# A Fourier mixing layer and a maxout FFN on one core: batches 0 and 1 in a new order, yb read in 4 transfers, last stores on two queues

## The chip, the cores and the metric

The kernel runs on one core of a Trainium2 chip. The metric is device time in microseconds (us). TensorE is called PE, its weight loads PEld; VectorE is DVE, ScalarE is ACT, GpSimd is POOL, SyncE is SP. A line such as L344 is a line of the kernel before.

## What is computed

```python
X = np.fft.fft(x, axis=1)            # x: (8, 3072, 256), float32
X = np.fft.fft(X, axis=2)
t = X.real.reshape(8 * 3072, 256)
h = np.maximum(np.maximum(t @ w1, t @ w2), t @ w3)   # w1, w2, w3: 256 x 768
out = h @ w_out                                      # w_out: 768 x 256
```

Eight batches of 3072 rows; the weights are shared.

## The kernel before, in words

Everything is written out in one order for each engine by hand (`manual_schedule`, L67); the framework adds only the waits. Each engine, and each engine's queue of DMA issues, works strictly in that order. A DMA also waits for the DMA eight before it of its kind, whose semaphore it takes over.

**Mixing.** The class `Mix` (L332) turns one batch of x into two bf16 tables tE and tO (128 x 1536), the even and odd parts of the transform along the sequence.
- `load_x` (L106) fetches x into one of two tiles xt, from POOL's queue, which also casts float32 to bf16; `mirror` (L113) then copies the reversed columns to partitions 64 to 127 with two DVE copies (L116, L117).
- `s(k)` (L340), k = 0 to 6: two matmuls with the small table tabz (L344; L348 for k = 6), evicted into tb (L346, L350).
- `y` (L352) stores tb to a DRAM tile db, in two or more pieces, two DMAs each. `z` (L361) reads it back transposed into yb: three parts, two column sets, and for each one DMA for row 48 and one for rows 0 to 47, so 12 DMAs. There is one yb; a read waits for all use of the batch before.
- `x0` (L375) computes a small correction x0s, and `c` (L384) copies it into yb (L385), after the reads have landed; on POOL, except for the first copy of batch 0, which is on ACT.
- `k(which, g)` (L387): matmuls of yb with the tables te_tab or to_tab (L395), evicted into tE (which = 0, called kE) or tO (kO) (L397). kO needs `c`, kE does not. `end` (L399) adds the last column.

**FFN.** gE, gO, gD are products of the DFT along the features and the weights (`product` L278, `keep_product` L290), so the FFN starts from tE and tO. A batch has 18 units: 3 blocks of 512 columns by 6 slices of the hidden width. In a unit `unit_plus` (L406) runs four 128x512 matmuls into two banks (L412, L413), `unit_out` (L423) takes the maximum of three (ACT stmp L426, DVE hp L427), and one unit later `unit_minus` (L416, L420) adds the gD products and a second `unit_out` gives hm. The second layer of a block (`l2_block`, L440; matmuls L436, L459, sum on DVE L464) is spread over the next six units; half of its rows go out with an indirect DMA on POOL (L469), half with DMAs on SP (L476). The last block has a form of its own, `l2_last` (L479), stored at L509.

**Order.** Before the units comes a start written line by line (L129 to L594): tables on POOL, DVE and ACT, batch 0's x in four chunks (FIRST, L127), its mixing, the first half of the products, and dummy matmuls `warm_up` (L555) that keep PE busy. From then on the dictionary `plan` (L623) says which mixing step runs behind which unit: `at(b, unit, fn)`. `fetch` and `turn` are loads and mirrors of a later batch; `ahead0`, `ahead1` and `ahead` (L671 to L677) place the steps of batch 1, batch 2 and the later ones within the units of the batch before. Before the change the start and the plan have it so:

```python
    for ch in range(4):
        at(0, (7, 8, 10, 11)[ch], lambda ch=ch: turn(1, ch))
        at(0, (12, 13, 14, 15)[ch], lambda ch=ch: fetch(2, ch))
        at(1, (1, 2, 3, 4)[ch], lambda ch=ch: turn(2, ch))
...
    ahead0 = {8: ("s0", "s1"), 9: ("s2", "y0"), 11: ("s3", "s4"), 12: ("s5", "s6", "y1", "x"),
              13: ("z",), 16: ("c",), 17: ("kE0", "kO0"), 20: ("kE1",), 21: ("kO1",),
              24: ("kE2",), 25: ("kO2", "end")}
```

Weights: `load_w(0)` (L252) is issued on POOL after the tables and fetches the first half of w1, w2, w3; `load_w(1)`, wout and batch 1's x follow after the fourth read of yb (L588 to L594).

Of the kernel before, what the change touches and what calls it, by code (L numbers as in the profile page):

```python
# [9 lines left out]
FP32 = mybir.dt.float32  # L10
# [33 lines left out]
def kernel(  # L44
# [9 lines left out]
    nc = tc.nc  # L54
# [77 lines left out]
    arv = ang_r.rearrange("p (k r) -> p k r", r=RI)  # L132
# [4 lines left out]
    dvec = gen.tile([128, 128], FP32, tag="dvec")  # L137
    iota(dvec, [[1, 128]])
    for i in range(2):
        nc.gpsimd.memset(xt[i][32:64, 0::48, :], 0.0)  # L140
    for (s0, s1) in FIRST:
        for h in range(2):
            load_x(0, s0, s1, h)

    kvec = gen.tile([128, NHALF + 1], FP32, tag="kvec")
    kv = kvec[:, 0:NHALF].rearrange("p (g c) -> p g c", g=3)
    for g in range(3):
# [10 lines left out]
         base=S + 1023, cm=-32)  # L158

# [4 lines left out]
    nc.vector.memset(yb, 0.0)  # L164
# [4 lines left out]
    half = gen.tile([128, 256], FP32, tag="half")  # L169
    nc.vector.memset(half[:, 0:128], 64.0)  # L170
    nc.vector.memset(half[:, 128:256], 0.0)

# [68 lines left out]

    def load_w(jh, after=None):
        ld = None
        for wsrc, wdst in ((moe_w1, w1_bf), (moe_w2, w2_bf), (moe_w3, w3_bf)):
            ld = nc.gpsimd.dma_start(
                out=wdst.rearrange("p (fc j) -> p fc j", fc=2)[:, :, jh * 384:(jh + 1) * 384],
                in_=wsrc.rearrange("(fc p) j -> p fc j", fc=2)[:, :, jh * 384:(jh + 1) * 384])
            if after is not None:
                tc.add_manual_dep(ld.ins, after.ins.name, AFTER, reason="others first")
        return ld  # L250

    load_w(0)  # L252

    scal(sgn, pidx, 0.0, ALU.is_equal)
    scal(sgn, sgn, 2.0, ALU.mult, -1.0, ALU.add)
    scal(dif, sgn, 1.0, ALU.subtract)
    angles(0, 512)
    mirror(0, *FIRST[1])
    nc.gpsimd.memset(x0s, 0.0)

    rows_v = rows_f.rearrange("p (b r) -> p b r", r=12)
    adj = gen.tile([128, 12], FP32, tag="adj")
    adv = adj.rearrange("p (g u) -> p g u", u=4)
    three = pidx.to_broadcast([128, 3])
    for u in (1, 2, 3):
        scal(adv[:, :, u], three, float(128 - 32 * u), ALU.is_ge, 3071.0, ALU.mult)
    low = gen.tile([128, 4], FP32, tag="low")
    for i, (edge, value) in enumerate(((31.0, -1023.0), (16.0, -1520.0), (32.0, -522.0),
                                       (32.0, -1541.0))):
        scal(low[:, i:i + 1], pidx, edge - 0.5, ALU.is_le, value, ALU.mult)  # L270
    scal(adv[:, 0, 0:1], low[:, 0:1], -32.0, ALU.add)
    nc.vector.tensor_tensor(out=adv[:, 1, 0:1], in0=low[:, 1:2], in1=low[:, 2:3], op=ALU.add)
    dve(out=adv[:, 2, 0:1], in_=low[:, 3:4])
    nc.vector.tensor_tensor(out=rows_v, in0=rows_v,
                            in1=adj.unsqueeze(1).to_broadcast([128, B, 12]), op=ALU.add)
    dve(out=rows_m, in_=rows_f)
# [55 lines left out]
    class Mix:  # L332
# [28 lines left out]
        def z(self, parts=(0, 1, 2), engs=(nc.sync, nc.sync)):  # L361
            spans = {0: ((0, 6, 0), (1, 6, 17)), 1: ((6, 12, 6), (6, 11, 22)),
                     2: ((12, 17, 12), (12, 17, 27))}
            done = []
            for part in parts:
                for cs in range(2):
                    (i0, i1, c0) = spans[part][cs]
                    c1 = c0 + i1 - i0
                    for (a, z) in ((48, NS), (0, 48)):
                        done.append(engs[cs].dma_start(  # L370
                            out=yb[cs * 64 + a:cs * 64 + z, i0 * 256:i1 * 256],
                            in_=self.db[a:z, c0 * 256:c1 * 256]))
            return done
# [13 lines left out]
        def k(self, which, g):  # L387

            special = {0: [(0, 0, 32)], 1: [(0, 0, 16), (16, 16, 16)], 2: [(16, 0, 32)]}[g]
            parts = [(5 * g + 1 + i, 32 + 96 * i, 96) for i in range(5)] + special  # L390
            tab = (te_tab, to_tab)[which]
            ps2 = ps_f.tile([128, 512], FP32, name="ps2", tag="ps")
            for (r, c0, wd) in parts:
                at = 11 if r == 16 else r if r < 11 else r + 1
                nc.tensor.matmul(ps2[:, c0:c0 + wd], ybv[:, at, which, :],  # L395
                                 tab[:, g * 512 + c0:g * 512 + c0 + wd], start=True, stop=True)
            nc.scalar.copy(out=(self.tE, self.tO)[which][:, g * 512:(g + 1) * 512], in_=ps2)  # L397
# [81 lines left out]
    def l2_last(hp, hm, te, to, flipped):  # L479
# [3 lines left out]
        for sub in (3, 0, 1, 2):  # L483
# [23 lines left out]
            for k, (p0, p1, row, c) in enumerate(stores):  # L507
                eng = nc.scalar if sub == 2 and k < 2 else nc.sync
                stored(eng.dma_start(out=out[row: row + 32 * (p1 - p0 - 1) + 1: 32, :],  # L509
                                     in_=ot[p0:p1, c:c + 256]), "direct", ("scattered",))  # L510
# [52 lines left out]
    nc.scalar.activation(out=md_all, in_=vm, func=AX.Sin, scale=float(2.0 * math.pi / 256.0))  # L563
    nc.scalar.activation(out=nmd_all, in_=vm, func=AX.Sin, scale=float(-2.0 * math.pi / 256.0))
# [3 lines left out]
    mirror(0, *FIRST[2])  # L568
    tables(0, 512)
    warm_up(4)  # L570
    m.s(4, pool=ps_s, evict=dve)
    m.y(32, 40)
    mirror(0, *FIRST[3])
    m.s(5, pool=ps_s)
    m.s(6, pool=ps_s, evict=dve)
    m.y(40, NS, engs=(nc.sync, nc.scalar))
# [48 lines left out]
    def at(b, unit, fn):  # L625
        plan.setdefault((b + unit // UNITS, unit % UNITS), []).append(fn)
# [27 lines left out]
    for (u, fn) in ((0, lambda: tables(1024, NHALF + 1)), (0, lambda: m.c(6, RI)),  # L654
                    (1, prep_some), (2, prep_some), (2, prep_some), (2, prep_some),
                    (3, lambda: m.k(0, 1)), (3, prep_some), (4, lambda: m.k(1, 1)),
                    (4, prep_some), (5, prep_some), (5, prep_some),
                    (7, lambda: m.k(0, 2)), (8, lambda: m.k(1, 2)), (8, m.end)):
# [12 lines left out]
    ahead0 = {8: ("s0", "s1"), 9: ("s2", "y0"), 11: ("s3", "s4"), 12: ("s5", "s6", "y1", "x"),  # L671
              13: ("z",), 16: ("c",), 17: ("kE0", "kO0"), 20: ("kE1",), 21: ("kO1",),
              24: ("kE2",), 25: ("kO2", "end")}
    ahead1 = {3: ("s0", "s1"), 4: ("s2", "y0", "s3"), 5: ("s4", "s5"), 6: ("s6", "y1", "x"),
              9: ("z",), 12: ("c",), **late}
    ahead = {1: ("s0", "s1"), 2: ("s2", "y0", "s3"), 3: ("s4", "s5"), 4: ("s6", "y1", "x"),
             7: ("z",), 11: ("c",), **late}  # L677
    for b in range(B - 1):
        for u, whats in (ahead0, ahead1, ahead)[min(b, 2)].items():
            for what in whats:  # L680
                at(b, u, lambda b=b, what=what: piece(b + 1, what))
# [75 lines left out]
```

## Time and profile before

| what | us |
|---|---|
| median of 3 runs (lowest, highest) | 450.39 (447.83, 450.78) |
| the profiled execution | 451.0 |
| its span, first to last instruction | 449.2 |
| PE busy in the span | 406.6 (91%) |
| DVE, ACT, POOL busy | 296.1, 255.2, 155.1 |
| mean granted PE clock | 0.984 |

The span is what the views divide; 1.8 us of the execution lie outside it. "Busy" of PE counts modelled ends of pipelined matmuls. A line of the timeline gives start, duration, engine, line of the kernel, operation, tiles (out<-in) and shape, and in brackets the idle time ahead of it with what ended it. "SPq", "ACTq" and "POOLq" are the queues' issues, which do not count as busy; "x12" means twelve instructions merged in one line, whose duration runs from the first start. The wait list gives total us, how often, and the longest.

### The profile page before, as it was taken

What the parts mean: (1) busy time and instruction counts of PE and PEld (TensorE: products, weight loads), DVE (VectorE), ACT (ScalarE), POOL (GpSimd) and SP (SyncE); (2) the same over time, 40 slices, a digit from 0 to 9 for tenths busy, and PEclk for the clock granted to TensorE, in tenths of its full rate; (3) what the DMA queues carried; (4) which work ended last, traced back from release to release, by engine and by line L of the source; (5) the groups of instructions that cost most, each with busy time, mean ns of one, the idle gap of its engine ahead of it and who ended that gap; (6) DMA issues with size and microseconds to landing.
All of it is one profiled execution on the core that took longest, in us unless ns stands there. A gap on an engine that the chain in (4) does not pass through costs nothing.

```text
span 449.2 us, 8328 instructions
## 1 busy us (share of the span) xinstructions
PE 406.6 (91%) x2768; PEld 250.8 (56%) x2768; DVE 296.1 (66%) x527; ACT 255.2 (57%) x481; POOL 155.1 (35%) x263
## 2 busy tenths in 40 slices
PE   1488889599987999999998999999999999999994
PEld 0144555355654666665665566665666566656663
DVE  6766775447564767685677667676669577666772
ACT  1457556247654665666656665666566755745540
POOL 9145033222252214531435125332443233214330
PEclk9999999869998999999999999999999999999999
DMA  7849246912496236943397257924693354312323
GB/s 105 132 105 193 36 101 132 209 38 80 92 189 139 70 98 143 207 110 84 98 187 160 73 137 153 183 90 103 146 205 92 83 132 123 91 49 59 85 82 107
DMA packets 68875, 52.79 MB, mean 118 GB/s; under 512 B 35816, under 2 KB 62960, under 8 KB 68320
## 3 DMA queue, kind: packets, MB, share of 16 engines
q0 software_dynamic: 23856, 26.28, 29.7%
q1 hardware_dynamic: 44544, 25.78, 22.7%
q8 instruction: 22, 0.36, 0.4%
q10 hardware_dynamic: 432, 0.20, 0.2%
q14 instruction: 21, 0.17, 0.1%
HBM read 34.73 MB, written 31.59 MB: 148 GB/s over the span
## 4 chain that ended last, share of the span: by engine, by line
PE 70%; DMA 11%; DVE 7%; issue 4%; ACT 3%; SPq 2%; POOL 1%; DVEq 0%; ACTq 0%; POOLq 0%
PE po L436 22%; PE pse L412 12%; PE pse L420 11%; PE pse L413 11%; DMA yb<-db 5%; PE ps L344 5%; PE po L459 3%; DMA xt<-in_x_dram 3%; DMA out_dram<-ot 3%; ACT stmp L426 2%; DVE hm L427 2%; PE pl L451 2%; PE ps L395 2%; SPq L476 1%; DVE ot L464 1%
## 5 line engine op out<-in xcount | busy, mean ns | idle before, releaser
L426 ACT ACTIVATE stmp<-pse 128x512 bf16<-128x512 f32 x288 | 170.1, 600 | 85.9 <-PE pse L413 73.7
L469 POOL DMA_INDIRECT out_dram<-ot,rows_m x92 | 105.4, 1146 | 234.2 <-DVE ot L464 219.2
L427 DVE TENSOR_TENSOR hp<-pse,stmp 128x512 bf16<-128x512 f32 x144 | 99.6, 691 | 114.8 <-PE pse L420 70.7
L412 PE MATMUL pse<-tE,gE 128*128 128x512 bf16 x288 | 110.0, 382 | 3.1 <-DVE hm L427 2.4
L413 PE MATMUL pse<-tO,gO 128*128 128x512 bf16 x288 | 110.0, 382 | 0.1
L427 DVE TENSOR_TENSOR hm<-pse,stmp 128x512 bf16<-128x512 f32 x144 | 99.1, 688 | 9.2 <-ACT stmp L426 8.2
L436 PE MATMUL po<-wout_bf,hp 128*128 128x256 bf16 x576 | 87.3, 275 | 0.0
L420 PE MATMUL pse<-tO,gD 128*128 128x512 bf16 x288 | 86.6, 382 | 0.0
L436 PE MATMUL po<-wout_bf,hm 128*128 128x256 bf16 x576 | 78.6, 273 | 0.0
L436 PEld LDWEIGHTS <-hp 128*128 128x128 bf16 x576 | 57.0, 99 | 27.0 <-issue 0.5
L436 PEld LDWEIGHTS <-hm 128*128 128x128 bf16 x576 | 56.4, 98 | 16.3
L464 DVE TENSOR_TENSOR ot<-po,even 128x512 f32<-128x512 f32 x92 | 62.9, 684 | 0.2
L420 PEld LDWEIGHTS <-gD 128*128 128x128 bf16 x288 | 27.8, 98 | 32.3 <-issue 0.5
L344 PE MATMUL ps<-xt,tabz 128*128 128x512 bf16 x96 | 27.5, 403 | 18.7 <-DVE xt L117 17.8
L346 ACT CAST tb<-ps 128x512 bf16<-128x512 f32 x47 | 25.9, 588 | 30.5 <-PE ps L344 30.5
L413 PEld LDWEIGHTS <-gO 128*128 128x128 bf16 x288 | 28.2, 98 | 26.5 <-issue 5.9
L412 PEld LDWEIGHTS <-gE 128*128 128x128 bf16 x288 | 28.2, 98 | 23.0 <-issue 1.7
L459 PE MATMUL po<-gw,tO 128*128 128x512 bf16 x92 | 35.4, 385 | 0.0
L397 ACT CAST tO<-ps 128x512 bf16<-128x512 f32 x24 | 14.1, 586 | 24.0 <-PE ps L395 12.9
L455 ACT COPY even<-pl 128x512 f32<-128x512 f32 x46 | 26.9, 585 | 0.9 <-PE pl L451 0.9
L116 DVE COPY xt<-xt 64x1524 bf16<-64x1524 bf16 (+4 forms) x32 | 19.1, 596 | 9.4 <-DMA xt<-in_x_dram 5.6
L397 ACT CAST tE<-ps 128x512 bf16<-128x512 f32 x24 | 14.1, 587 | 19.4 <-PE ps L395 19.4
(132 smaller groups left out, 233.6 us busy)
## 6 DMA issues: line engine op xcount, KB each, us to landing
out_dram<-ot SPq DMA_DIRECT2D x75, 96.0 KB
xt<-in_x_dram POOLq DMA_DIRECT2D x14, 384.0 KB
db<-tb SPq DMA_DIRECT2D x21, 192.0 KB
yb<-db SPq DMA_DIRECT2D x32, 120.0 KB
out_dram<-ot SPq DMA_DIRECT2D x48, 64.0 KB
xt<-in_x_dram POOLq DMA_DIRECT2D x7, 400.0 KB
xt<-in_x_dram POOLq DMA_DIRECT2D x7, 368.0 KB
yb<-db SPq DMA_DIRECT2D x16, 144.0 KB
```

The costliest lines, as they stand in the source:

```text
L344: nc.tensor.matmul(ps1, tab_at[hh], self.x[:, 8 * k + hh:8 * k + 8:2, 0:128], start=(hh == 0), stop=(hh == 1))
L397: nc.scalar.copy(out=(self.tE, self.tO)[which][:, g * 512:(g + 1) * 512], in_=ps2)
L412: nc.tensor.matmul(pse[:, 0:n], gE[i][:, js], te, start=True, stop=False)
L413: nc.tensor.matmul(pse[:, 0:n], gO[i][:, js], to, start=False, stop=True)
L420: nc.tensor.matmul(pse, gD[i][:, js], to, start=False, stop=True, skip_group_check=True)
L426: nc.scalar.activation(out=stmp[:, 0:n], in_=pses[0][:, 0:n], func=AX.Relu)
L427: nc.vector.tensor_tensor(out=dst, in0=src3, in1=stmp[:, 0:n], op=ALU.max)
L436: nc.tensor.matmul(po, hcols(jc), wout_bf[:, jc * 256:(jc + 1) * 256], start=False, stop=(jc == NJC - 1), skip_group_check=True)
L455: nc.scalar.copy(out=even, in_=pl)
L459: nc.tensor.matmul(po, to[:, cp], gw[:, 256:768], start=True, stop=True)
L464: nc.vector.tensor_tensor(out=ot.rearrange("p (h c) -> p h c", h=2), in0=po.rearrange("p (h c) -> p h c", h=2), in1=lin.unsqueeze(1).to_br ...
L469: stored(nc.gpsimd.indirect_dma_start(out, bass.IndirectOffsetOnAxis(ap=rows_m[0:128 - lo, b * 12 + slot: b * 12 + slot + 1], axis=0), ot[ ...
```

## The change

Seven things, all in order or grouping; the matmuls of the units stay as they are.

1. ang_r is filled by two iotas instead of four (yb now has its columns in natural order); the zeroing of two columns of xt moves from POOL to DVE; dvec's iota moves behind the first chunk's loads; the zeroing of yb moves on DVE to just before the first mirror.
2. Both halves of the weights are issued on POOL right behind x: the first ahead of the kvec tables, the second behind them.
3. On DVE the mirrors of batch 0's chunks come as x lands: chunk 1 ahead of the par and reduction steps, chunks 2 and 3 ahead of the first `angles`; the rows_m steps move behind the last `angles`. On ACT, md_all and nmd_all come behind the fifth S eviction.
4. `warm_up` uses xt and tabz instead of md_all: 3, 3, 3, 4 and 6 matmuls instead of 4, 8 and 12. The last db stores of batch 0 both go on SP.
5. Only wout (with batch 1's x behind it) waits for the fourth read of yb.
6. `z` reads yb in one part, 4 DMAs (batch 0: two parts, 8 DMAs; its first four as before). Batch 1's steps move up, and batch 2 follows the plan of the later batches; `ahead1` is gone.
7. In `l2_last` the stores alternate between SP and ACT.

The diff, cut to its core:

```diff
-    iota(arv[:, :, 0:11], [[0, 4], [1, 11]])
-    iota(arv[:, :, 11], [[0, 4]], base=16)
-    iota(arv[:, :, 12:17], [[0, 4], [1, 5]], base=11)
-    iota(arv[:, 1, 0:15], [[1, 15]], base=1)
...
+    iota(ang_r, [[0, 4], [1, RI]])
+    iota(ang_r[:, RI:2 * RI], [[1, RI]], base=1)
     for i in range(2):
-        nc.gpsimd.memset(xt[i][32:64, 0::48, :], 0.0)
+        nc.vector.memset(xt[i][32:64, 0::48, :], 0.0)
...
+    load_w(0)
...
+    load_w(1)
...
+    nc.vector.memset(yb, 0.0)
+    nc.gpsimd.memset(x0s, 0.0)
     mirror(0, *FIRST[0])
...
+    mirror(0, *FIRST[1])
...
-        def z(self, parts=(0, 1, 2), engs=(nc.sync, nc.sync)):
-            spans = {0: ((0, 6, 0), (1, 6, 17)), 1: ((6, 12, 6), (6, 11, 22)),
-                     2: ((12, 17, 12), (12, 17, 27))}
+        def z(self, parts=(2,)):
+            spans = {0: ((0, 6, 0), (1, 6, 17)), 1: ((6, 17, 6), (6, 16, 22)),
+                     2: ((0, 17, 0), (1, 16, 17))}
...
-                eng = nc.scalar if sub == 2 and k < 2 else nc.sync
+                eng = (nc.sync, nc.scalar)[k % 2]
...
+    mirror(0, *FIRST[2])
+    mirror(0, *FIRST[3])
+    angles(0, 512)
...
-    landed = m.z()
-    warm_up(8)
+    tables(0, 512)
+    landed = m.z((0, 1))
     angles(512, 1024)
-    tables(512, 1024)
+    warm_up(4)
...
-    warm_up(12)
+    warm_up(6)
+    tables(512, 1024)
     angles(1024, NHALF + 1)
-    load_w(1, landed[3])
...
-        at(0, (7, 8, 10, 11)[ch], lambda ch=ch: turn(1, ch))
-        at(0, (12, 13, 14, 15)[ch], lambda ch=ch: fetch(2, ch))
-        at(1, (1, 2, 3, 4)[ch], lambda ch=ch: turn(2, ch))
+        at(0, (4, 5, 6, 7)[ch], lambda ch=ch: turn(1, ch))
+        at(0, (13, 14, 15, 16)[ch], lambda ch=ch: fetch(2, ch))
+        at(0, (17, 18, 19, 20)[ch], lambda ch=ch: turn(2, ch))
...
-    ahead0 = {8: ("s0", "s1"), 9: ("s2", "y0"), 11: ("s3", "s4"), 12: ("s5", "s6", "y1", "x"),
-              13: ("z",), 16: ("c",), 17: ("kE0", "kO0"), 20: ("kE1",), 21: ("kO1",),
-              24: ("kE2",), 25: ("kO2", "end")}
-    ahead1 = {3: ("s0", "s1"), 4: ("s2", "y0", "s3"), 5: ("s4", "s5"), 6: ("s6", "y1", "x"),
-              9: ("z",), 12: ("c",), **late}
+    ahead0 = {5: ("s0", "s1"), 6: ("s2", "y0"), 7: ("s3", "s4"), 9: ("s5", "s6", "y1", "x"),
+              12: ("z",), 15: ("c",), 16: ("kE0",), 17: ("kO0",), 19: ("kE1",), 20: ("kO1",),
+              21: ("kE2",), 22: ("kO2", "end")}
     ahead = {1: ("s0", "s1"), 2: ("s2", "y0", "s3"), 3: ("s4", "s5"), 4: ("s6", "y1", "x"),
              7: ("z",), 11: ("c",), **late}
```

More of the change, by code (lines that the diff above doesn't have):

```diff
@@ L131, with load_w @@
     ang_r = gen.tile([128, 4 * RI], FP32, tag="ang_r")
-    arv = ang_r.rearrange("p (k r) -> p k r", r=RI)
-    iota(arv[:, :, 0:11], [[0, 4], [1, 11]])
-    iota(arv[:, :, 11], [[0, 4]], base=16)
-    iota(arv[:, :, 12:17], [[0, 4], [1, 5]], base=11)
-    iota(arv[:, 1, 0:15], [[1, 15]], base=1)
-    dvec = gen.tile([128, 128], FP32, tag="dvec")
-    iota(dvec, [[1, 128]])
+    iota(ang_r, [[0, 4], [1, RI]])
+    iota(ang_r[:, RI:2 * RI], [[1, RI]], base=1)
     for i in range(2):
-        nc.gpsimd.memset(xt[i][32:64, 0::48, :], 0.0)
-    for (s0, s1) in FIRST:
+        nc.vector.memset(xt[i][32:64, 0::48, :], 0.0)
+    for c, (s0, s1) in enumerate(FIRST):
         for h in range(2):
             load_x(0, s0, s1, h)
+        if c == 0:
+            dvec = gen.tile([128, 128], FP32, tag="dvec")
+            iota(dvec, [[1, 128]])
+    def load_w(jh):
+        for wsrc, wdst in ((moe_w1, w1_bf), (moe_w2, w2_bf), (moe_w3, w3_bf)):
+            nc.gpsimd.dma_start(
+                out=wdst.rearrange("p (fc j) -> p fc j", fc=2)[:, :, jh * 384:(jh + 1) * 384],
+                in_=wsrc.rearrange("(fc p) j -> p fc j", fc=2)[:, :, jh * 384:(jh + 1) * 384])
+    load_w(0)
     kvec = gen.tile([128, NHALF + 1], FP32, tag="kvec")
@@ L168 @@
     nc.vector.memset(ang_o[:, 3 * RI:4 * RI], 24.0)
-    half = gen.tile([128, 256], FP32, tag="half")
-    nc.vector.memset(half[:, 0:128], 64.0)
-    nc.vector.memset(half[:, 128:256], 0.0)
     def small(name):
@@ L203 @@
     dve = nc.vector.tensor_copy
+    nc.vector.memset(yb, 0.0)
+    nc.gpsimd.memset(x0s, 0.0)
     mirror(0, *FIRST[0])
+    half = gen.tile([128, 256], FP32, tag="half")
+    nc.vector.memset(half[:, 0:128], 64.0)
+    nc.vector.memset(half[:, 128:256], 0.0)
     vm = gen.tile([128, 512], FP32, tag="vm")
@@ L240, in tables @@
                              bias=half_pi)
[L242 to L276, printed above, removed]
     def product(i, half, jh, pool, tag):
@@ L369, in z @@
                     for (a, z) in ((48, NS), (0, 48)):
-                        done.append(engs[cs].dma_start(
+                        done.append(nc.sync.dma_start(
                             out=yb[cs * 64 + a:cs * 64 + z, i0 * 256:i1 * 256],
@@ L393, in k @@
             for (r, c0, wd) in parts:
-                at = 11 if r == 16 else r if r < 11 else r + 1
-                nc.tensor.matmul(ps2[:, c0:c0 + wd], ybv[:, at, which, :],
+                nc.tensor.matmul(ps2[:, c0:c0 + wd], ybv[:, r, which, :],
                                  tab[:, g * 512 + c0:g * 512 + c0 + wd], start=True, stop=True)
@@ L556, in warm_up @@
         for _ in range(n):
-            nc.tensor.matmul(warm, md_all[:, 0:128], md_all, start=True, stop=True)
+            nc.tensor.matmul(warm, tab_at[0], xt[0][:, 0:8:2, 0:128], start=True, stop=True)
+    mirror(0, *FIRST[2])
+    mirror(0, *FIRST[3])
+    angles(0, 512)
+    scal(sgn, pidx, 0.0, ALU.is_equal)
+    scal(sgn, sgn, 2.0, ALU.mult, -1.0, ALU.add)
+    scal(dif, sgn, 1.0, ALU.subtract)
     m = Mix(0)
@@ L562 @@
     m.y(0, 16)
-    nc.scalar.activation(out=md_all, in_=vm, func=AX.Sin, scale=float(2.0 * math.pi / 256.0))
-    nc.scalar.activation(out=nmd_all, in_=vm, func=AX.Sin, scale=float(-2.0 * math.pi / 256.0))
+    warm_up(3)
     m.s(2, pool=ps_s)
@@ L567 @@
     m.y(16, 32)
[L568 to L571, printed above, removed]
+    warm_up(3)
+    m.s(4, pool=ps_s)
     m.y(32, 40)
-    mirror(0, *FIRST[3])
+    nc.scalar.activation(out=md_all, in_=vm, func=AX.Sin, scale=float(2.0 * math.pi / 256.0))
+    nc.scalar.activation(out=nmd_all, in_=vm, func=AX.Sin, scale=float(-2.0 * math.pi / 256.0))
+    warm_up(3)
     m.s(5, pool=ps_s)
     m.s(6, pool=ps_s, evict=dve)
-    m.y(40, NS, engs=(nc.sync, nc.scalar))
+    m.y(40, NS)
     m.x0()
-    landed = m.z()
-    warm_up(8)
+    tables(0, 512)
+    landed = m.z((0, 1))
     angles(512, 1024)
-    tables(512, 1024)
+    warm_up(4)
     for half in range(2):
@@ L585 @@
         keep_product(product(1, half, 0, ps_s, "ps"), 1, half, 0, dve)
-    warm_up(12)
+    warm_up(6)
+    tables(512, 1024)
     angles(1024, NHALF + 1)
-    load_w(1, landed[3])
+    rows_v = rows_f.rearrange("p (b r) -> p b r", r=12)
+    adj = gen.tile([128, 12], FP32, tag="adj")
+    adv = adj.rearrange("p (g u) -> p g u", u=4)
+    three = pidx.to_broadcast([128, 3])
+    for u in (1, 2, 3):
+        scal(adv[:, :, u], three, float(128 - 32 * u), ALU.is_ge, 3071.0, ALU.mult)
+    low = gen.tile([128, 4], FP32, tag="low")
+    for i, (edge, value) in enumerate(((31.0, -1023.0), (16.0, -1520.0), (32.0, -522.0),
+                                       (32.0, -1541.0))):
+        scal(low[:, i:i + 1], pidx, edge - 0.5, ALU.is_le, value, ALU.mult)
+    scal(adv[:, 0, 0:1], low[:, 0:1], -32.0, ALU.add)
+    nc.vector.tensor_tensor(out=adv[:, 1, 0:1], in0=low[:, 1:2], in1=low[:, 2:3], op=ALU.add)
+    dve(out=adv[:, 2, 0:1], in_=low[:, 3:4])
+    nc.vector.tensor_tensor(out=rows_v, in0=rows_v,
+                            in1=adj.unsqueeze(1).to_broadcast([128, B, 12]), op=ALU.add)
+    dve(out=rows_m, in_=rows_f)
     wld = nc.gpsimd.dma_start(out=wout_bf.rearrange("p (jc c) -> p jc c", jc=NJC),
                               in_=moe_w_out.rearrange("(jc p) c -> p jc c", jc=NJC))
+    tc.add_manual_dep(wld.ins, landed[3].ins.name, AFTER, reason="others first")
     HALVES = ((0, 25), (25, NS))
@@ L652, in turn @@
         mirror(b, *CHUNKS[ch])
-    for (u, fn) in ((0, lambda: tables(1024, NHALF + 1)), (0, lambda: m.c(6, RI)),
-                    (1, prep_some), (2, prep_some), (2, prep_some), (2, prep_some),
-                    (3, lambda: m.k(0, 1)), (3, prep_some), (4, lambda: m.k(1, 1)),
+    for (u, fn) in ((0, prep_some), (0, prep_some), (0, lambda: m.c(6, RI)),
+                    (0, lambda: tables(1024, NHALF + 1)), (1, prep_some), (1, prep_some),
+                    (2, lambda: m.k(0, 1)), (2, lambda: m.k(1, 1)), (3, prep_some),
                     (4, prep_some), (5, prep_some), (5, prep_some),
@@ L678 @@
     for b in range(B - 1):
-        for u, whats in (ahead0, ahead1, ahead)[min(b, 2)].items():
+        for u, whats in (ahead0, ahead)[min(b, 1)].items():
             for what in whats:
```

1 line of the change is left out of this document (removed).

## The prediction, made before the result

> **What bounds the kernel now.** I read the page's slices of the span first. TensorE (PE) is full except in three places: the first stretch, two dips near 86 and 137 us, and the end.
>
> ```profile
> PE   1488889599987999999998999999999999999994
> PEclk9999999869998999999999999999999999999999
> ```
>
> The table by stage puts numbers on them. After the stage's own length it gives busy us of PE, weight loads, DVE, ACT and POOL, and then the granted clock.
>
> ```profile
> 0.00:32.00 32.00, 14.54 (x68) 6.45 (x69) 22.50 (x78) 11.55 (x23) 15.52 (x36) 1.00 0.66 116
> 48.70:84.00 35.30, 32.98 (x215) 19.91 (x212) 24.30 (x41) 21.34 (x41) 12.44 (x18) 1.00 0.52 107
> 84.00:96.70 12.70, 6.51 (x30) 3.45 (x31) 2.07 (x4) 2.85 (x5) 1.34 (x3) 0.60 0.59 121
> 132.40:144.50 12.10, 7.44 (x52) 4.32 (x51) 5.00 (x10) 4.44 (x8) 1.45 (x4) 0.86 0.77 163
> 144.50:436.00 291.50, 289.20 (x2022) 181.49 (x2020) 203.49 (x334) 181.45 (x342) 102.44 (x171) 1.00 0.49 117
> ```
>
> From 144.5 to 436 PE idles 2.3 us of 291.5. The change adds no PE work there and takes none away, so only the other stages can give. PE's waits name who ended the idle time (total, times, longest):
>
> ```profile
> PE ps L344 <- DVE xt L117: 17.8, 5, 9.9
> PE ps L395 <- POOL yb L385: 6.9, 2, 3.5
> PE ps L395 <- DMA yb<-db: 4.0, 2, 2.7
> PE psg L284 <- DMA w_bf<-in_moe_w_dram: 1.4, 1, 1.4
> ```
>
> The timeline of the start shows why:
>
> ```profile
> 16.67 0.69 DVE L116 COPY xt<-xt 64x2032 bf16<-64x2032 bf16 x1
> 22.57 0.49 DVE L116 COPY xt<-xt 64x1143 bf16<-64x1143 bf16 x1
> 24.44 0.67 ACTq L358 DMA_DIRECT2D db<-tb  x1
> 26.82 4.20 SPq L370 DMA_DIRECT2D yb<-db  x12
> 30.74 0.22 ACT L385 COPY yb<-x0s 128x6 bf16<-128x6 bf16 x1 [1.65 <-DMA yb<-db]
> 31.98 0.38 PE L412 MATMUL pse<-tE,gE 128*128 128x512 bf16 x1 [0.44 <-ACT tE L397]
> ```
>
> The trace's completion marks put batch 0's four chunks of x at 8.57, 11.79, 13.10 and 14.67. Yet the mirrors of chunks 1 and 3 run at 16.67 and 22.57: x is there, and DVE's order is what is late. From the last mirror a serial chain (S, eviction, store to db, read to yb) leads to the first FFN matmul at 31.98. At the first handover, batch 0 to 1:
>
> ```profile
> 76.45 10.40 SPq L370 DMA_DIRECT2D yb<-db  x12
> 86.66 0.58 PE L395 MATMUL ps<-te_tab,yb 128*128 128x96 bf16 x6 [2.71 <-DMA yb<-db]
> 90.46 0.26 POOL L385 COPY yb<-x0s 128x17 bf16<-128x17 bf16 x1 [6.83 <-DMA out_dram<-ot]
> 90.78 0.61 PE L395 MATMUL ps<-to_tab,yb 128*128 128x96 bf16 x6 [3.53 <-POOL yb L385]
> ```
>
> The read's 12 issues take SP 10.40 us, against 4.20 for batch 0. They share the DMA engines with batch 2's fetch, and PE waits 2.71 and 3.53. The clock then stands at 0.5 until 96.6 (a 128x512 matmul starts every 0.427 us instead of 0.215). The tail is one queue:
>
> ```profile
> 438.38 8.30 SPq L509 DMA_DIRECT2D out_dram<-ot  x14
> 442.97 0.42 DVE L501 COPY ot<-po 128x256 f32<-128x256 f32 x1 [0.52 <-PE po L436]
> ```
>
> DVE is done at 443.39, but SP issues until 446.69.
>
> **The sum, part by part.** It is made against the profiled execution: 451.0 us, span 449.2; the median of the three runs is 450.39, 0.6 below.
>
> *1. First FFN matmul.* The first load of x leaves POOL at 2.89. Ahead of it go two of four iotas (half of 0.75), dvec (0.25) and two memsets (0.98): 1.6 earlier, and the chunks land at about 7.0, 10.2, 11.5 and 13.1. On DVE, the yb memset (1.87) and `half` leave the front, so the table work ending at 8.36 ends at 6.3. The two xt memsets that DVE takes over, 0.3 each at the rate of the yb memset, lie under ACT's table load (0.74 to 2.02). The yb memset now stands before the first mirror, 6.3 to 8.2; chunk 0 is there, so that mirror starts at 8.2 instead of 8.69, ending at 9.4. Then DVE in its new order: `half` and vm 1.6, mirror 1 0.8, par and the reduction 2.9, mirror 2 0.5, mirror 3 0.6, to 15.8 (was 23.14); angles 2.2, sgn 0.4 and the eviction of S6 0.3, to 18.7. ACT's eviction of S5 stands behind the two md tables (1.15), near 18.0. The last two db stores leave SP at 18.7 and 19.3 (they left SP and ACT together at 24.4); a lone one landed 2.5 after issue, so 21.8. Both weight halves are now on the DMA engines behind x: x moved its 1.5 MB in 8.3 us, so 2 x 0.59 MB after 13.1 end near 20 to 21. A db store issued at 12.48 into such a backlog needed 6.5. Bounds for the last store: 21.8 and 25.8; I take 22.1, since it is issued when the backlog is nearly gone. From the first read issue to the yb copy 3.9, from there to the first matmul 1.24: **27.2, that is -4.8** (bounds -5.1 and -0.9). rows_m and the other angles run under this chain on DVE, done about 26.3, before the first hp near 28.7.
>
> *2. Clock at the first units.* S and the warm-ups keep PE busy from 9.5; the products follow near 18 and end at 20.6, six warm-ups at 21.9; the k matmuls start near 26. A gap of 4 us is longer than the 2.7 us that preceded the drop at 86.4. Half clock lasted 3.4 us (141.0 to 144.4) and 10.2 us (5.8 of it busy). Cost 0 to 2.9; ACT limits part of those units, so **+1.5**.
>
> *3. Second weights.* The wait of 1.40 goes. But ACT now evicts gO ahead of its last table, 1.9 us long, and the third unit needs that ACT: -1.4 to +1.0, **-0.7**.
>
> *4. Batch 1's x and S.* Its loads wait for the first reads of yb (25.8) and for wout: four at 1.9 each, as before, land from 32 to 38. The mirrors stand on DVE at about 37, 39, 41 and 44, ahead of hp; cover 2 to 3 us. If it were gone, DVE and then PE would stop for the difference. S waited 2.0 in all around units 8 to 12, and will wait the same at 5 to 9, behind gw now: **0** (-0.5 to +1).
>
> *5. First handover.* 2.71 + 3.53 of waiting and half of 5.8 + 0.6 busy us at half clock, 9.4 in all. y1 now comes three units before the read; the read is 4 issues on SP (1.3 us at 0.3 each), queued ahead of batch 2's fetch on POOL. Units 13 and 17 began at 71.86 and 81.41, so 4.8 earlier at 67.1 and 76.6. The read leaves by 67 and moves the same 0.75 MB, which took 6.3 us alone (26.82 to 33.14): it lands near 73, ahead of the copy behind unit 15 (about 74 to 76) and of kO behind unit 17 (79). **-8.9** (all gone less 0.5; at worst 6 stay).
>
> *6. Second handover.* 1.30 + 3.36 of waiting and half of 3.4: 6.4. Batch 1 gets the steady plan, in which later handovers waited 0.3 to 1.3 in the old kernel. What is late next is batch 2's x: its fetch (5 to 9 us to land) is four units ahead of its mirror, 10.6 us at 2.66 a unit. **-5.4** (bounds -2.4 and -6.4).
>
> *7. Later handovers.* 2.1 us of waiting for DVE hm; a shorter read frees SP's stores and POOL's scatters earlier, both queued behind it. **-0.7** (-2.1 to +1).
>
> *8. Tail.* Eight stores to a queue. The last pair leaves at 443.5 on SP and ACT, takes 0.5 to issue and 2.0 to land, like the ACT stores at 443.06: 446.0, against 448.13. ACT's last activation began at 435.70, so nothing waits behind its issues. **-2.2** (-1.3 to -2.4).
>
> The Trainium skill (DMA: Bandwidth & Descriptors, "Issuing engines are not separate DMA queues") says that a second issuing engine saves only the sequencer's issue time, usually little beside the transfer. By that rule term 8 would be near 0 and the sum 432. The trace disagrees here: the 8.30 us on SP are issue time, and they outlast the data.
>
> Sum: -4.8 +1.5 -0.7 +0 -8.9 -5.4 -0.7 -2.2 = -21.2. 451.0 - 21.2 = **429.8**, rounded to 430.0.
>
> **The rivals.**
>
> *A, the first handover stays in part.* For it: batch 2's fetch still follows the read within a few us, and under that mix a read took 13.8 us (76.45 to 90.23). Against: y1 has landed long before, and the read is queued whole. With 6 of the 9.4 us left: 435.5.
>
> *B, the start gains nearly nothing.* The db stores land only when both weight halves are through (6.5 us as at 12.48), the first matmul is at 31.1: 3.9 lost, 434.
>
> *C, slower.* A read of whole rows of 8.7 KB could run badly, in every batch. In the steady plan the read is issued after unit 7, and kO comes after unit 14: 18.6 us of room. The old reads took 9.7 to 13.4. To eat the 21 us, seven handovers must lose 3 each, a wait of 1.3 and 1.7 of slow clock; the read would have to take about 20 us, and 21 or more to be slower by over 1%. Nothing in the trace shows long rows to be slow; near 457 if so.
>
> *D, it does not do what it says.* Batch 0 keeps 8 reads, its first four as before, so "4 transfers" does nothing for the start; my start does not count on it. That the stalls move elsewhere whole: about 450.
>
> **How the numbers follow.** Forecast (425 to 434) 0.62, A 0.15, B 0.13, C 0.07, D 0.03. Faster by over 1% (about what a measurement can tell) are the forecast, A and B: 0.90; within 1% D: 0.03; slower C: 0.07. Low end: all terms at their better bounds give 423.7, all at once being unlikely, so 425. High end: A with part of B's loss, 437; beyond stand C, D and A with B whole, under 0.2.
>
> **What would show it.** Right: the last chunk's mirror by 16 and the first gE matmul by 28; no PE gap over 1 us before the odd matmuls of batches 1 and 2, and clock 1.0 through both handovers; PE's end to the span's end about 4 us instead of 6.3. Wrong: db<-tb landing after 24 (B), ps<-to_tab still waiting for POOL's yb copy (A), DVE's mirrors of batch 1 or 2 waiting for x (terms 4, 6), yb<-db over 15 us in every batch (C).

## The result, and the profile after

| | before | after |
|---|---|---|
| median, us (lowest to highest, 4 runs each) | 450.58 (447.83 to 454.12) | 429.49 (428.9 to 430.16) |
| ratio, 95% interval | | 0.9528 [0.9459, 0.9597] |
| span of the profiled execution | 449.2 | 428.0 |
| mean granted PE clock | 0.984 | 0.996 |

The predicted time was 430.0. Line numbers below are those of the kernel after: L317 is S (before L344), L331 the stores to db (L358), L343 the read of yb (L370), L358 the copy `c` (L385), L367 `k` (L395), L384 and L385 the first matmuls of a unit (L412, L413), L399 hp and hm (L427), L481 the last stores (L509).

The slices of the span: the two dips of PE and of its clock are gone. What is left is the start (6 to 8 tenths up to 64 us), one slice of 8 near 123 us, and the end.

```profile
PE   1768789999989999999999999999999999999996
PEclk9989999999999999999999999999999999999999
```

PE's waits (total, times, longest). Nothing waits for POOL's yb copy any more, and the 2.7 of yb is one wait, in the start:

```profile
PE ps L317 <- DVE xt L117: 12.8, 4, 8.8
PE pse L384 <- DVE hm L399: 3.3, 6, 1.4
PE ps L367 <- DMA yb<-db: 2.7, 1, 2.7
PE psw L296 <- DVE g1t L291: 1.4, 1, 1.4
```

The start in the timeline. The last long mirror runs at 15.73 (22.57 before), the first FFN matmul at 26.46 (31.98):

```profile
6.03 1.87 DVE L206 MEMSET yb<- 128x2176 uint32 x1 [0.39 <-issue]
10.31 1.03 DVE L116 COPY xt<-xt 64x2032 bf16<-64x2032 bf16 x1
15.73 0.48 DVE L116 COPY xt<-xt 64x1143 bf16<-64x1143 bf16 x1
21.72 2.86 SPq L343 DMA_DIRECT2D yb<-db  x8
25.36 0.22 ACT L358 COPY yb<-x0s 128x6 bf16<-128x6 bf16 x1 [1.65 <-DMA yb<-db]
25.40 0.39 PE L367 MATMUL ps<-te_tab,yb 128*128 128x96 bf16 x6 [2.71 <-DMA yb<-db]
26.46 0.58 PE L384 MATMUL pse<-tE,gE 128*128 128x512 bf16 x1 [0.30 <-ACT tE L369]
```

The first handover. Four issues in 1.34 us, and neither k (te_tab for kE, to_tab for kO) has a wait in brackets. Six of their matmuls take 0.39 us (0.58 and 0.61 before, at half clock); the granted clock is 1.00 here:

```profile
67.59 1.34 SPq L343 DMA_DIRECT2D yb<-db  x4
77.64 0.39 PE L367 MATMUL ps<-te_tab,yb 128*128 128x96 bf16 x6
77.94 0.27 POOL L358 COPY yb<-x0s 128x17 bf16<-128x17 bf16 x1
80.26 0.39 PE L367 MATMUL ps<-to_tab,yb 128*128 128x96 bf16 x6
```

And the tail. Two queues issue side by side and are through at 425.41, 1.2 us behind PE's end at 424.19 (before: 446.69, 3.8 behind 442.93). From PE's end to the span's end it is 3.84 us, before 6.29:

```profile
419.64 5.51 SPq L481 DMA_DIRECT2D out_dram<-ot  x8
419.64 5.77 ACTq L481 DMA_DIRECT2D out_dram<-ot  x8
424.23 0.42 DVE L473 COPY ot<-po 128x256 f32<-128x256 f32 x1 [0.52 <-PE po L408]
```

Where the 21.2 us of the span came from, cut at the first hp of each batch (the DVE maximum that ends a first unit):

| stretch | before | after | difference |
|---|---|---|---|
| span's start to first hp | 33.51 | 28.49 | -5.02 |
| batch 0, first hp to batch 1's first | 60.54 | 54.21 | -6.33 |
| batch 1 | 57.94 | 52.14 | -5.80 |
| batches 2 to 7, to the last hp | 282.2 | 280.6 | -1.6 |
| last hp to span's end | 15.1 | 12.6 | -2.5 |

Two parts of the change stand neither in the list of seven nor in the diff shown with it. Batch 0's own steps move up in the plan: half of the remaining products by one or two units, the first kE of the plan by one, the first kO by two. And ACT, not DVE, evicts S4. Only e5 below undoes them, together with the start.

### The profile page after: what moved, and what is told of

Its sections match the earlier page's. It is cut to its first block, busy times and chain, and to the rows that moved or that the text cites. A ratio compares the mean times of both kernels' runs of the same rounds, so it can differ in the third digit from the quotient of the medians.

```text
span 428.0 us, 8171 instructions
## 1 busy us (share of the span) xinstructions
PE 397.9 (93%) x2715; PEld 248.8 (58%) x2763; DVE 295.2 (69%) x528; ACT 255.5 (60%) x482; POOL 153.7 (36%) x259
## 4 chain that ended last, share of the span: by engine, by line
PE 75%; DMA 9%; DVE 8%; issue 4%; ACT 3%; SPq 0%; POOL 0%; DVEq 0%; POOLq 0%; ACTq 0%
PE po L408 25%; PE pse L384 14%; PE pse L392 12%; PE pse L385 11%; DMA xt<-in_x_dram 7%; PE ps L317 4%; PE po L431 4%; PE pl L423 2%; DVE hm L399 2%; PE ps L367 2%; ACT stmp L398 1%; DMA out_dram<-ot 1%; DVE hp L399 1%; DVE xt L116 1%; DVE ot L436 1%
## 5 line engine op out<-in xcount | busy, mean ns | idle before, releaser
L399 DVE TENSOR_TENSOR hp<-pse,stmp 128x512 bf16<-128x512 f32 x144 | 99.5, 691 | 108.3 <-PE pse L392 66.6
L384 PE MATMUL pse<-tE,gE 128*128 128x512 bf16 x285 | 108.1, 379 | 6.4 <-DVE hm L399 3.3
L399 DVE TENSOR_TENSOR hm<-pse,stmp 128x512 bf16<-128x512 f32 x144 | 98.9, 687 | 1.1 <-ACT t_mid L376 0.7
L385 PE MATMUL pse<-tO,gO 128*128 128x512 bf16 x252 | 95.9, 380 | 0.5 <-issue 0.4
L408 PE MATMUL po<-wout_bf,hp 128*128 128x256 bf16 x576 | 86.1, 273 | 0.1
L392 PE MATMUL pse<-tO,gD 128*128 128x512 bf16 x280 | 83.9, 379 | 0.3
L385 PEld LDWEIGHTS <-gO 128*128 128x128 bf16 x288 | 28.1, 98 | 27.9 <-issue 7.7
L384 PEld LDWEIGHTS <-gE 128*128 128x128 bf16 x288 | 28.1, 97 | 22.5 <-issue 1.1
L317 PE MATMUL ps<-xt,tabz 128*128 128x512 bf16 x96 | 26.7, 390 | 13.4 <-DVE xt L117 12.8
L431 PE MATMUL po<-gw,tO 128*128 128x512 bf16 x91 | 34.5, 379 | 0.0
L427 ACT COPY even<-pl 128x512 f32<-128x512 f32 x46 | 27.0, 586 | 0.1
L111 POOL DMA_DIRECT2D xt<-in_x_dram x36 | 23.4, 661 | 0.0
```

What stands on the lines that cost most here:

```text
L317: nc.tensor.matmul(ps1, tab_at[hh], self.x[:, 8 * k + hh:8 * k + 8:2, 0:128], start=(hh == 0), stop=(hh == 1))
L384: nc.tensor.matmul(pse[:, 0:n], gE[i][:, js], te, start=True, stop=False)
L385: nc.tensor.matmul(pse[:, 0:n], gO[i][:, js], to, start=False, stop=True)
L392: nc.tensor.matmul(pse, gD[i][:, js], to, start=False, stop=True, skip_group_check=True)
L399: nc.vector.tensor_tensor(out=dst, in0=src3, in1=stmp[:, 0:n], op=ALU.max)
L408: nc.tensor.matmul(po, hcols(jc), wout_bf[:, jc * 256:(jc + 1) * 256], start=False, stop=(jc == NJC - 1), skip_group_check=True)
```

## The experiments

Three theories of the handovers stood against each other. Theory 1: the order counts (when the read is issued, and what is in the DMA engines with it). Theory 2: few transfers cure the handovers in any order. Theory 3: the number of transfers does nothing. All kernels below are the changed one with one edit, unless said. Behind each median stand its ratio to the kernel before, run beside it, and the 95% interval. The kernel before had medians of 451.31 beside e1 to e4, 451.78 beside e5 to e8, 451.72 beside e9 and e10, 452.86 beside e11 and e12, and 450.58 above. So a difference of up to some 2 us between medians of two of these groups settles nothing by itself.

**12 transfers in the new order** (e1).

```diff
-        def z(self, parts=(2,)):
+        def z(self, parts=(0, 3, 4)):
...
```

> The changed kernel with batches 1 to 7 read in 12 transfers again; all else as changed. Theory 1 (the order is what counts: y1 three units before the read, the read ahead of the fetch): the 12 issues spread over 4 to 10 us and mix with the fetch, so the read of batch 1 lands some 4 us later than its 7 us, still before kO; 430 to 432. Theory 2 (few transfers are the cure of the handovers): the stall at the first handover comes back with 3 us or more, the later ones too, 436 to 443. Theory 3 (the number does nothing at all): 429 to 430.

430.39 us, 0.9567 [0.9505, 0.9629]; span 428.0, the same as with 4.

```profile
67.95 4.43 SPq L344 DMA_DIRECT2D yb<-db  x12
78.06 0.39 PE L368 MATMUL ps<-te_tab,yb 128*128 128x96 bf16 x6
```

No wait: theory 2's stall did not come. The read took 6.5 us at the first handover and 9.6 to 11.1 later (7.1 to 8.1 with 4), all of it hidden: in this order the number is worth nothing that shows.

**4 transfers in the old order** (e2: the kernel before, with yb in natural order and 4 transfers for batches 1 to 7; batch 0 keeps 12).

```diff
...
-        def z(self, parts=(0, 1, 2), engs=(nc.sync, nc.sync)):
+        def z(self, parts=(2,), engs=(nc.sync, nc.sync)):
...
-    landed = m.z()
+    landed = m.z((0, 3, 4))
```

> The kernel before with yb in natural order and batches 1 to 7 read in 4 transfers; batch 0's reads, the start, the plan and the last stores as before. Theory 1: the read of batch 1 still leaves at 76.5, behind y1, beside the fetch; 10 us of issue become 1.3, PE's 6.2 us of waiting at the first handover shrink to 2 to 4 and the second's 4.7 to 1 to 2; 442 to 446. Theory 2: both stalls go, 435 to 438. Theory 3: 449 to 451.

442.76 us, 0.982 [0.9775, 0.9864].

```profile
76.37 1.31 SPq L368 DMA_DIRECT2D yb<-db  x4
87.61 0.58 PE L392 MATMUL ps<-te_tab,yb 128*128 128x96 bf16 x6 [3.79 <-DMA yb<-db]
88.03 0.59 PE L392 MATMUL ps<-to_tab,yb 128*128 128x96 bf16 x6
```

PE's waits for the read (total, times, longest):

```profile
PE ps L392 <- DMA yb<-db: 7.1, 2, 3.8
```

So the number does count here, against theory 3: two waits a handover became one, and the time fell by some 8 us. In the profile 5.6 of them lie in batches 0 and 1, 1.0 in batches 2 to 7, and 1.6 in the tail, where this edit changes nothing (see e4). Why 12 were worse: of the old kernel's twelve issues the last left at 86.54, since the DMA eight before it, issued at 77.46, landed at 86.53. But waits of 3.79 and 3.34 stay, against theory 2; the second is longer than theory 1 had it.

**The old plan in the new kernel** (e3: places of `turn`, `fetch`, `ahead0` and `ahead1` as before the change; start, 4 transfers and tail new).

```diff
-        at(0, (4, 5, 6, 7)[ch], lambda ch=ch: turn(1, ch))
-        at(0, (13, 14, 15, 16)[ch], lambda ch=ch: fetch(2, ch))
-        at(0, (17, 18, 19, 20)[ch], lambda ch=ch: turn(2, ch))
+        at(0, (7, 8, 10, 11)[ch], lambda ch=ch: turn(1, ch))
+        at(0, (12, 13, 14, 15)[ch], lambda ch=ch: fetch(2, ch))
+        at(1, (1, 2, 3, 4)[ch], lambda ch=ch: turn(2, ch))
...
+              13: ("z",), 16: ("c",), 17: ("kE0", "kO0"), 20: ("kE1",), 21: ("kO1",),
...
```

> The changed kernel with the places of batch 1's and 2's steps as before (turn, fetch, ahead0, ahead1); start, 4 transfers and last stores as changed. Theory 1: the first read leaves right behind y1, at unit 13, beside the fetch; PE waits 2 to 4 us at unit 17 and 1 to 2 in batch 1, with the slow clock behind the first; 434 to 438. Theory 2: no more than 431, since the 4 transfers are still there.

439.36 us, 0.972 [0.9667, 0.9773]; a little above theory 1's range, far above theory 2's.

```profile
73.72 1.31 SPq L343 DMA_DIRECT2D yb<-db  x4
86.11 0.59 PE L367 MATMUL ps<-te_tab,yb 128*128 128x96 bf16 x6 [4.93 <-DMA yb<-db]
```

The places are worth some 10 us. Against e2 the read leaves 2.65 earlier, and the wait grows by 1.14: the stall gives back part of what the start gained.

**What in the places does it.** e11 moves only batch 2's loads of x in the changed kernel, e12 only the same loads in e3's.

```diff
# e11
-        at(0, (13, 14, 15, 16)[ch], lambda ch=ch: fetch(2, ch))
+        at(0, (11, 12, 13, 14)[ch], lambda ch=ch: fetch(2, ch))
# e12
-        at(0, (12, 13, 14, 15)[ch], lambda ch=ch: fetch(2, ch))
+        at(0, (14, 15, 16, 17)[ch], lambda ch=ch: fetch(2, ch))
```

> The changed kernel, with only batch 2's four loads of x moved two units earlier in the plan (behind units 11 to 14 instead of 13 to 16), so that two of them are queued ahead of the first handover's read of yb, as in the order before. What does the new plan cure the handover by? Theory 'sharing': the read is short (7.2 us) because no load of x is in the DMA engines with it; now it takes 10 to 12 us and lands at 78 to 80, up to 2 us behind the k matmuls' place at 77.64; PE waits up to 2 us there and the time is 430 to 433. Theory 'earlier': the read is simply issued 6 us earlier; it keeps its place, no wait appears, 429 to 430.

432.04 us, 0.9561 [0.9513, 0.9608].

```profile
78.94 0.39 PE L367 MATMUL ps<-te_tab,yb 128*128 128x96 bf16 x6 [0.88 <-DMA yb<-db]
```

> The old plan in the changed kernel (439.36 us, waits of 4.93 and 3.54 us at the handovers), with only batch 2's four loads of x moved two units later (behind units 14 to 17), so that they are queued behind the first handover's read of yb. Theory 'sharing': the read, issued at about 73.7 us, takes 7.5 to 9 us instead of 12.1 and lands near 82 instead of 85.9; the first handover's wait of 4.93 shrinks to 0.5 to 2 and the time falls to 434 to 437. Theory 'earlier': what the old plan lacks is an earlier issue; the wait stays at 4 to 5 us, 438.5 to 440.

438.27 us, 0.9705 [0.9641, 0.977].

```profile
84.57 0.39 PE L367 MATMUL ps<-te_tab,yb 128*128 128x96 bf16 x6 [3.74 <-DMA yb<-db]
```

e11 came out as theory 'sharing' had it. e12 fell between the two: its wait of 3.74 and its time lie just below what 'earlier' expected, and well above what 'sharing' did. Both theories hold a part. All first handovers with one-part reads, and e1, set side by side (room: from the read's first issue to where PE would have started kE, that is its start less its wait; length: from first issue to the last completion mark; in every row further loads of x were issued 4 to 7 us into the read):

| kernel | read issued | room | length | loads of x issued near its start | wait |
|---|---|---|---|---|---|
| after | 67.59 | 10.05 | 7.19 | none, first at 72.57 | 0 |
| e1, 12 transfers | 67.95 | 10.11 | 6.5 | none, first at 73.01 | 0 |
| e11 | 68.75 | 9.31 | 10.06 | 65.69, 68.17 | 0.88 |
| e12 | 73.39 | 7.44 | 10.93 | 73.22 | 3.74 |
| e3 | 73.72 | 7.46 | 12.14 | 73.59, 74.36 | 4.93 |
| e2 | 76.37 | 7.45 | 11.10 | 76.23, 77.00 | 3.79 |

Where there is a wait it is length less room within 0.3 us. The new plan gives 2.6 us more room and takes the loads out of the read's way, which makes it 3 us shorter (e11 against after). The room alone nearly does (e11's 0.88). Whether the free read alone does is open: e12's first load still left 0.17 ahead of the read, so a read without loads was not seen in the old room, which it would just fit (7.2 in 7.4). By the ratios e11 is 1.5 to 2.5 us slower than the changed kernel (0.9528 above, 0.9505 as e10 below), and its wait explains 0.9 of that; in the profiled execution (431.06) another 0.8 is a later first hp, which the edit does not touch.

The second handover goes the same way. In e2, e3 and e12 the room is 7.91 and the length 11.2 to 11.5, and PE waits 3.34, 3.54 and 3.71; in the changed kernel the room is 12.5 and the length 7.8. Which of the moved steps makes that room, no run separates.

**The old last stores** (e4).

```diff
-                eng = (nc.sync, nc.scalar)[k % 2]
+                eng = nc.scalar if sub == 2 and k < 2 else nc.sync
```

> The changed kernel with the last stores as before: 14 on SP, 2 on ACT. Term 8: from PE's end to the span's end 6.2 us again instead of 3.8; 431.5 to 432.2. Rival (a second queue saves nothing, since the data share the same DMA engines): 429.5 within 0.5.

431.43 us, 0.9558 [0.9517, 0.9598]; PE's end to the span's end 4.95, against 3.84 after and 6.29 before.

```profile
420.06 6.71 SPq L481 DMA_DIRECT2D out_dram<-ot  x14
424.17 1.21 ACTq L481 DMA_DIRECT2D out_dram<-ot  x2
```

SP issues until 426.77, 1.4 past the changed kernel's last issue. Term 8 had expected 6.2 us from PE's end here. So the second queue is worth 1.1 us by the profile; by the medians 1.0 against e1 beside it, and 1.9 against the first result. The other 1.3 of the tail's gain are not its work: in the kernel before, one of the 14 issues on SP (at 439.67) took 1.69 us, where the others took 0.32 to 0.60. Neither e4 nor e2 had such an issue with the same stores (6.71 and 6.69 us for the 14, against 8.30). What held it up is open.

**The old start** (e5: the start and batch 0's own steps as before the change, with yb in natural order; plan of the later batches, 4 transfers and tail new).

```diff
...
-    load_w(0)
...
-    load_w(1)
...
-    mirror(0, *FIRST[1])
...
+    angles(0, 512)
+    mirror(0, *FIRST[1])
...
+    mirror(0, *FIRST[2])
+    tables(0, 512)
...
+    mirror(0, *FIRST[3])
...
+    load_w(1, landed[3])
...
```

> The kernel before's start (POOL, DVE, ACT and warm-up order up to the first unit, second weights late, batch 0 read in 12 transfers) with the changed plan of batches 1 and 2, 4 transfers for batches 1 to 7 and the changed last stores. If the gains add up (theory 1): the first hp is at 33.4 again instead of 28.5, the handovers stay clean, so 433.5 to 436. Rival (the handovers are clean only because the start is early): a stall of 2 us or more in batch 0 or 1, 437 or more.

433.55 us, 0.9602 [0.9557, 0.9647]; first hp at 33.36, batch 0 54.36, batch 1 51.66, and no wait at a handover. The start, with batch 0's own steps, is worth some 4 us, and the handovers' gain does not hang on it.

**18 warm-ups instead of the last 6** (e6).

```diff
-    warm_up(6)
+    warm_up(18)
```

> The changed kernel with 18 warm-up matmuls instead of 6 ahead of the first yb matmuls. Term 2: the 2.7 us of PE idle before them shrink to 0.2 or less, the granted clock stays 1.0 from 12 us on, and the first units get 1.0 to 1.7 us shorter: 427.8 to 428.5. Rival (ACT limits those units whatever the clock): the clock stays up and the time does not move, 429.2 to 429.8.

429.44 us, 0.9515 [0.9472, 0.9557]. By stage, first after, then e6 (length; busy PE, weight loads, DVE, ACT, POOL; clock):

```profile
22.50:25.80 3.30, 0.59 (x11) 0.43 (x11) 3.10 (x14) 1.39 (x3) 1.54 (x2) 1.00 0.63 181
25.80:29.20 3.40, 2.88 (x13) 1.28 (x12) 1.55 (x3) 1.67 (x3) 3.39 (x5) 0.50 0.67 103
```

```profile
22.50:25.80 3.30, 3.30 (x17) 1.38 (x15) 3.20 (x6) 1.94 (x4) 2.30 (x2) 1.00 0.45 120
25.80:29.20 3.40, 2.81 (x24) 1.59 (x24) 1.97 (x15) 1.89 (x4) 2.80 (x5) 1.00 0.68 132
```

The clock stays at 1.00, as term 2 had it, but the time does not move, as the rival had it. The profiles show what the half clock costs all the same. From the first FFN matmul to batch 1's first hp, the four with the drop and this batch 0 (after, e1, e4, e10) took 55.6 to 56.6 us, the two without it (e6, e7) 54.9: some 1.2 us. e6's total hides this, because its first FFN matmul came at 27.06, 0.6 later than in the changed kernel's profile. Chunk 1 of x landed at 10.85 there instead of 10.04, with nothing edited ahead of it; over the profiles with this start that matmul lies between 26.36 (e10) and 27.80 (e11).

The drop is not in every execution. Of the ten of the changed kernel (four above, six as e10), five had a mean clock of 0.999 or 1.000 and spans of 426.1 to 427.4; the other five (0.991 to 0.996) had 427.0 to 429.5.

**Mirrors late, second weights late** (e7: chunks 1 to 3 mirrored behind the first `angles`; e8: `load_w(1)` waits for the fourth read of yb, as before the change).

```diff
# e7
...
-    mirror(0, *FIRST[1])
...
+    angles(0, 512)
+    mirror(0, *FIRST[1])
     mirror(0, *FIRST[2])
     mirror(0, *FIRST[3])
-    angles(0, 512)
# e8
...
+            if jh == 1:
+                tc.add_manual_dep(ld.ins, landed[3].ins.name, AFTER, reason="others first")
...
-    load_w(1)
...
+    load_w(1)
...
```

> The changed kernel with the mirrors of batch 0's chunks 1 to 3 behind the first angles on DVE again. Term 1: the last mirror ends near 19.6 instead of 16.3, the last db store leaves 2.4 to 2.9 later and the first hp is at 31 to 31.5: 431.8 to 433. Rival (the start is earlier because x is fetched earlier and the yb memset is out of the way, not by the order of the mirrors): within 1 us of 429.5.

433.25 us, 0.9601 [0.9557, 0.9645]; first read of yb at 25.84 (21.72 after), first hp 32.35.

```profile
25.84 2.86 SPq L342 DMA_DIRECT2D yb<-db  x8
```

Time and first hp lie somewhat beyond what was expected. Of the 4.9 us between e5's first hp (33.36) and the changed kernel's (28.49), 3.9 are gone: most of the start's gain was DVE's order. Behind a PE gap of 5.32 us the clock also stood at 0.50 from 15.49 to 22.31 here; what that adds, no run separates.

> The changed kernel with the second half of the weights behind the fourth read of yb again. Term 3: the wait of 1.4 us in the first units comes back in part, 430 to 431; the last db stores land at the same 22.0. Rival (B: the weights behind x hold up the db stores): the db stores land 0.5 us or more sooner and the first hp moves up with them, 428.5 or less.

431.61 us, 0.956 [0.9511, 0.961], a little above what term 3 had; first hp 28.89, so rival B's gain did not come.

```profile
30.70 0.48 PE L259 MATMUL psg<-w_bf,md_all 128*128 128x384 bf16 x2 [1.92 <-DMA w_bf<-in_moe_w_dram]
```

The weights now end a wait of 1.92 on PE, and batch 0 takes 56.67. The stores to db landed sooner (the second pair at 18.06 and 18.52 instead of 20.42 and 21.11), but nothing waited for them: the last pair, issued 19 to 20, landed at 22.0 with the weights ahead and 22.37 without.

**A version beside the changed kernel** (e9 beside e10, the changed kernel again; 6 runs each).

```diff
-            nc.vector.tensor_copy(out=g1t[:, jp * 512:(jp + 1) * 512], in_=pst)
+            nc.scalar.copy(out=g1t[:, jp * 512:(jp + 1) * 512], in_=pst)
...
-    warm_up(6)
+    warm_up(18)
...
-        at(0, (4, 5, 6, 7)[ch], lambda ch=ch: turn(1, ch))
+        at(0, (4, 4, 5, 6)[ch], lambda ch=ch: turn(1, ch))
```

> A version meant to take out the three waits of the changed kernel's first batch that stand on VectorE: 1.37 us before the weight product at 42.9 (g1t L291 on VectorE), 1.04 and 0.74 us at 45.7 and 53.2 (mirror copies of batch 1, L117). The evictions of the second weights go to ScalarE, batch 1's mirrors come one unit earlier (its halves had landed at 34.96 and 40.05), and 18 warm-up matmuls stand in place of 6. If VectorE is what limits units 2 to 5, most of the 3.15 us go: 425.5 to 427.5. Rival: the work only moves, ScalarE then limits the same units (its waits stand in their place), 429 to 429.8, as the changed kernel.

> The changed kernel once more, as the yardstick for the run beside it: 429 to 430 by every theory.

e9: 427.27 us (426.28 to 428.18), 0.9463 [0.9435, 0.9492]; e10: 428.79 (427.84 to 431.23), 0.9505 [0.9471, 0.9539]. PE's waits in e9:

```profile
PE ps L317 <- DVE xt L117: 11.2, 3, 9.1
PE ps L317 <- ACT gw L302: 0.9, 1, 0.9
PE psw L296 <- ACT g1t L291: 0.2, 1, 0.2
```

The 1.37 for g1t fell to 0.24, the two waits for mirrors went, and in their places S waits 0.86 and 0.23 for ACT: of 3.15 us 1.33 are left, now ACT's. Theory and rival both hold a part. Batches 0 and 1 together took 102.9, against 106.6; 1.3 came back in batch 3, with a wait of 1.19 before a unit's first matmul. The spans differ by 1.6 (425.4, 427.0), the medians by 1.5, but the intervals overlap: probably faster, by a third of a per cent, not settled.

## Why the prediction was right, point by point

- **Term 1, first FFN matmul** (predicted -4.8, bounds -5.1 and -0.9): -5.5, a little past its better bound. Chunks of x landed at 6.93, 10.04, 11.35 and 12.97 (predicted 7.0, 10.2, 11.5, 13.1), the last db store at 22.02 (22.1). The read's first transfer, row 48 alone, needed only the store ahead of that one (landed 21.66) and left at 21.72. From there to the yb copy it took 3.64 (3.9), from the copy to the matmul 1.10 (1.24). Rival B's mechanism was there and cost nothing: the pair of stores issued at 13.73 and 14.35 needed 6.7 us behind the weights, but the last pair needed 2.4 and 2.2.
- **Term 2, slow clock** (+1.5, bounds 0 and 2.9): about 1.2 by the profiles (e6), not seen in the medians. 0.5 of it lies ahead of the first hp, which came 2.03 us behind the first FFN matmul instead of 1.53. The gap was 2.7 us and not 4. The 5.8 busy us that the term quotes leave out 0.6 of k matmuls, which term 5 adds.
- **Term 3, second weights** (-0.7): the old wait of 1.40 is gone, and a new one of 0.75 for ACT (stmp) stands at 32.7, so -0.65. e8 has the early loads' own worth, 2.2 us in the median against e6 beside it.
- **Term 4, batch 1's x and S** (0, -0.5 to +1): +1.1, just past its upper bound. x landed from 33.00 to 40.05 (predicted 32 to 38). S and x0 waited 2.40 in all (2.05 before), of it 1.04 and 0.74 for mirrors (0.60 and 0.19); psw waited 1.37 for g1t (0.93), and one unit 0.35 for hm that did not before. All three are DVE's work: its cover was thinner than the 2 to 3 us assumed. e9 takes part of this away.
- **Terms 5 and 6, the handovers** (-8.9 and -5.4): right, and no rival of them came. The waits of 2.71, 3.53, 1.30 and 3.36 are gone and the clock is 1.00 from 29.2 to the end of the PE work. The read left at 67.6 (predicted by 67) and landed at 74.8 (73). Term 5 left 0.5 us of stall, and none came. Term 6 left 1.0 for the waits of the steady plan, and they came to 2.0: 1.36 for hm at 127.75, and 0.65 more in short waits around batch 2's S. From the first FFN matmul to batch 2's first hp the change gave -11.6 (120.01 to 108.38), where terms 2 to 6 sum to -13.5. The differences named make up 1.4 of these 1.9; the other 0.5 is less than repeats differ by (107.8 to 108.6 in after, e1, e4, e10).
- **Term 7, later handovers** (-0.7): -1.6, within its bounds, but not clear of chance: the same batches took 279.4 to 282.2 us in e10, e4 and e3, which all have the changed kernel's steps there. The reads take 7.1 to 8.1 instead of 9.6 to 13.3; e1, with reads of 9.6 to 11.1, has the same span, so the shorter read is not shown to be the cause.
- **Term 8, tail** (-2.2, bounds -1.3 and -2.4): -2.5 in the profile, but only half of it for the term's reason. The second queue gave 1.1 (e4), less than the term's worse bound. The rest is the one issue of 1.69 us, which is part of the 8.30 us that the term took for the price of these stores. That the number fits is luck. By the Trainium skill (DMA: Bandwidth & Descriptors, "Issuing engines are not separate DMA queues") only issue time is saved, usually little; the trace agrees that issue time is what was saved, but it was what ended last, and not little here.
- **Rival C** (long rows slow): not so; no read took over 8.1.

The sum came out at -21.2 both ways by luck in part. To the first FFN matmul, in batches 0 and 1, in batches 2 to 7 and in the tail it had -4.8, -13.5, -0.7 and -2.2; measured were -5.5, -11.6, -1.6 and -2.5. So 1.9 too much met 0.7, 0.9 and 0.3 too little.

Two edits overlap: from the kernel before, 4 transfers give about 8 us (e2), and the new places then another 8 to 10 (e5 against e2 less the tail, the changed kernel against e3); but with the new places in, 4 against 12 transfers give nothing (e1). Undoing parts one at a time therefore does not add up to the whole.

## What to carry to other kernels

For a transfer that ends a wait, set its length beside its room (from issue to first use by an engine that must not stop), and ask which other transfers are queued around it: moving a load behind it can be worth as much as making it shorter. A gain in the start is kept only if the next wait does not take it back (e3 against e2: the read 2.65 earlier, the wait 1.14 longer), so mend the handover first. Where two cures meet the same wait, test each with the other in place and without it.

## What the runs showed of the hardware

- The granted clock changed only in steps of 3.41 us. In the 14 profiles it fell from 1.00 to 0.50 behind the 16 steps in which PE was busy at most 1.3 us, and behind none in which PE was busy 1.45 us or more (the span's end left out). So it counts where a gap falls. The gap of 2.71 us (22.7 to 25.4) lay within one step, with 0.70 us of work, and 3.4 us at 0.50 followed, as behind e8's of 2.57 and the waits of 3.3 to 4.9 in e2, e3 and e12. e5's gap of 2.40 lay across the end of a step at 35.54; PE was busy 2.25 us in the one and 2.07 in the other, and no drop followed.
- The same read (784 KB) took 6.5 us in 12 transfers with the first load of x issued 5 us behind it (e1), and 13.8 with two issued beside it (before, its last transfer held back to 86.54); in 4 transfers 7.2 and 10 to 12.
- A store issued while weights were queued from POOL took 6.7 us, and 2.2 to 2.4 when the last of them landed at 20.92, 1 to 1.7 us behind its issue.
